# Attention with a running decay: the decay moved into the second score product, the mask into the row minimum

## The chip, the cores and the metric

The kernel runs on one core of a Trainium2 chip. The metric is the device time of one execution in microseconds, lower is better. The profile and the trace come from one execution of the kernel, taken by the hardware profiler. PE is the matrix engine (PEld its weight loads), DVE the vector engine, ACT the scalar engine, POOL is GpSimd, and SP issues DMAs.

## The reference

Attention over 2 batches, 8 heads, 576 positions and 64 channels, with a decay that is summed along the sequence, followed by two mixtures of experts. Only attention is touched by the change:

```python
scores = scale * np.matmul(q, k.transpose(0, 1, 3, 2))
causal = np.triu(np.ones((S, S), dtype=bool), k=1)
cum = np.cumsum(np.maximum(s, 0.0), axis=-1)
bias = -(cum[:, :, :, None] - cum[:, :, None, :])
scores = np.where(causal, -1000000000.0, scores + np.minimum(bias, 0.0))
scores = scores - np.max(scores, axis=-1, keepdims=True)
attn = np.exp(scores)
attn = attn / (np.sum(attn, axis=-1, keepdims=True) + 1e-09)
return np.matmul(attn, v)
...
```

The attention output is then routed to one of 8 experts per token (`_moe_ref`) and goes through 4 dense experts weighted by domain (`_moe2_ref`).

## The kernel before

Attention works in units (h, c, b): head h, block c of 128 queries, batch b. Blocks 0 to 3 see (c + 1) x 128 keys. Block 4 holds the last 64 queries of both batches together, and its 576 keys are cut into two units of 288. That makes 10 units a head and 80 in all, in the order of `ORDER` (`LAST` for head 7).

Everything is kept negated, so the softmax takes a row minimum. Products of float32 accuracy are made from the fast float32r form: q is split into a rounded part and a remainder that stand one above the other in 128 rows (`ql`, turned by PE into `qT`, or `qr` for block 4). k is turned into `kh` (rounded, twice one above the other) and `kl` (what the rounding lost). A unit's scores (`qk`) are two products of 128 rows into one PSUM tile `sc`, `kh` first and `kl` second. A third, bf16 product of an identity with `mkb` or `mrb` adds 1e9 above the diagonal (L209, L218).

The decay is a work of DVE in `nb`: `max(cum_j - cum_i, 0)` per unit from `bc` or `br`, the cumulated row broadcast to all 128 partitions by DMA from the DRAM tensor `ncum_d` (`loadbc`, `loadbr`), and a column per query from `ncT`/`ncR` (L231, L236). For head 0 `bc` is made by PE and ACT instead (L91, L92). `smin` adds scores and decay and takes the row minimum in one DVE instruction (L246). `expo` is the exponential on ACT, `pT` turns the weights on PE and evicts them on ACT to `ptT`, and `av` multiplies them with v (L283, L286, L288). `fin` divides.

The loop in `run` goes over step j and writes the stages of different units: row minimum of unit j+2, turning of j, parts of the next head's preparation (`prep_q`, `prep_k`, `prep_r` at set steps), scores of j+3, exponential of j+1, decay of j+3, value product of j-1. `load(h + 2)` and `loadbc(h + 2)` are written at step 4 of head h. The program's text doesn't fix the order on an engine: a list scheduler puts the instructions into each engine's queue by this order and by when it reckons them ready, and each queue is then worked off in order. `issue_after(x)` is an edge in that ordering, from x to the instructions on x's engine that are written inside it, with no wait on the chip. Buffers: two for scores (`SCB`), three in PSUM for turning (`ps_t`), two for what belongs to a head.

Of the kernel before, what the change touches and what calls it, by code (L numbers as in the profile page):

```python
# [42 lines left out]
class Attention:  # L43
# [6 lines left out]
    def __init__(self, ctx, tc, nc, ident, q, k, v, sp, X):  # L50
        self.tc, self.nc, self.q, self.k, self.v, self.X, self.ident = tc, nc, q, k, v, X, ident
        pool = lambda n, b, **kw: ctx.enter_context(tc.tile_pool(name=n, bufs=b, **kw))
# [3 lines left out]
        dram = pool("adram", 1, space=DRAM)  # L56
# [4 lines left out]
        self.L, self.U, self.last = {}, {}, [None, None]  # L61
# [5 lines left out]
        self.scr = dram.tile([B * H, S], F32, name="ncum_d")  # L67
# [8 lines left out]
        rows = []  # L76
        for b in range(B):
            rows.append(c.tile([16, P], F32, name=f"row{b}"))
            nc.vector.tensor_copy(out=rows[b], in_=ident[:16, 8 * b : 8 * b + 1].to_broadcast([16, P]))
        self.idb = c.tile([P, P], BF16, name="idb")  # L80
        self.ready = nc.vector.tensor_copy(out=self.idb, in_=ident)
        ncm = c.tile([16, S + 64], F32, name="ncm")
        with self.tc.issue_after(self.ready.ins):
            nc.vector.tensor_scalar(out=st, in0=st, scalar1=-1.0, scalar2=0.0, op0=ALU.mult, op1=ALU.min)
        nc.vector.tensor_tensor_scan(out=ncm[:, :S], data0=ones, data1=st, initial=0.0, op0=ALU.mult, op1=ALU.add)
# [3 lines left out]
        for b in range(B):  # L89
# [3 lines left out]
        mk = c.tile([P, P], F32, name="mk")  # L93
        nc.gpsimd.memset(mk, 0.0)
        nc.gpsimd.affine_select(out=mk, in_=mk, pattern=[[-1, P]], compare_op=ALU.is_ge, fill=1e9, base=0, channel_multiplier=1)
        z = c.tile([P, P], F32, name="zz")
        nc.gpsimd.memset(z, 0.0)
        self.mkb = c.tile([P, P], BF16, name="mkb")
        self.mrb = c.tile([P, 64], BF16, name="mrb")
        self.qr = [c.tile([P, 2, P], F32R, name=f"qr{i}") for i in range(2)]  # L100
        with self.tc.issue_after(scan.ins):
            nc.vector.tensor_copy(out=self.mkb, in_=mk)
            nc.vector.tensor_copy(out=self.mrb[0:64, :], in_=mk[0:64, 0:64])
            nc.vector.tensor_copy(out=self.mrb[64:128, :], in_=mk[64:128, 64:128])
            for t in self.qr:
                nc.vector.tensor_copy(out=t, in_=z.unsqueeze(1).to_broadcast([P, 2, P]))
        self.ncT = c.tile([P, 5, 16], F32, name="ncT")
        self.ncR = c.tile([P, 8], F32, name="ncR")
        pt = self.ps_t.tile([P, 512], F32, tag="pt", name="pt")
        for i in range(5):  # L110
            nc.tensor.transpose(out=pt[:, i * 16 : i * 16 + 16], in_=ncm[:, i * P : i * P + P], identity=ident[:16, :16])
        nc.vector.tensor_copy(out=self.ncT, in_=pt[:, :80].rearrange("p (c h) -> p c h", h=16))
        nc.vector.tensor_copy(out=self.ncR[0:64, :], in_=self.ncT[0:64, 4, 0:8])
        nc.vector.tensor_copy(out=self.ncR[64:128, :], in_=self.ncT[64:128, 4, 8:16])

    def warm(self, n):

        t = self.ps_t.tile([P, 512], F32, tag="pt", name="pt")
        for _ in range(n):
# [24 lines left out]
    def loadbc(self, h):  # L144
# [6 lines left out]
        if h:  # L151
            self.loadbr(h)
# [963 lines left out]
```

## Time and profile before

| | us |
|---|---|
| runs, median of 3 (lowest, highest) | 713.06 (712.0, 713.32) |
| the profiled execution, whole | 709.65 |
| its span, first to last instruction | 708.0 |
| PE busy | 682.5 |
| DVE busy | 444.8 |
| ACT busy | 332.1 |
| POOL busy | 166.8 |

The span is what the views of the trace divide up; the whole time has 1.65 us around it. Busy times are sums over the span, and engines work beside each other, so only the one that the others wait for sets the time in a stretch. Attention ends near 155 us, and the two mixtures fill the rest.

### The profile page before, as it was taken

How to read it: one execution, taken by the hardware profiler on the slowest of the kernel's cores; microseconds unless marked ns; L12 is line 12 of the kernel's file. 1: busy time of each engine (PE TensorE's matmuls, PEld its weight loads, DVE VectorE, ACT ScalarE, POOL GpSimd, SP SyncE). 2: the span in 40 equal slices, each digit the busy share in tenths (PEclk: the TensorE clock that was granted, in tenths of full speed). 3: DMA queues.
4: the chain of work that ended last, by engine and by line, in shares of the span. 5: the costliest groups of instructions: out<-in, count | busy, mean ns of one | idle time of the engine just before them, and what ended most of it. 6: DMA issues, size and time to landing. Idle time of an engine off the chain costs nothing.

```text
span 708.0 us, 12759 instructions
## 1 busy us (share of the span) xinstructions
PE 682.5 (96%) x4829; PEld 632.5 (89%) x4830; DVE 444.8 (63%) x1006; ACT 332.1 (47%) x617; POOL 166.8 (24%) x193
## 2 busy tenths in 40 slices
PE   8899999987999999998999999999999999999996
PEld 5789999876999999998989989899899898998995
DVE  7486868653117111367875876868758768687583
ACT  5476777631116111344826636438166364382640
POOL 2000000032400000011513632434126323351333
PEclk9899999978999999999999999999999999999999
DMA  6746557118998977310110111011101100112002
GB/s 139 196 111 187 147 159 172 44 75 267 361 325 293 331 246 236 124 60 4 61 60 1 61 60 32 29 60 61 60 2 60 59 32 29 61 60 60 1 31 104
DMA packets 87015, 78.92 MB, mean 111 GB/s; under 512 B 42699, under 2 KB 67275, under 8 KB 86951
## 3 DMA queue, kind: packets, MB, share of 16 engines
q1 hardware_dynamic: 83063, 72.76, 33.8%
q0 software_dynamic: 1776, 4.79, 1.8%
q10 hardware_dynamic: 2112, 0.52, 0.4%
q8 instruction: 39, 0.64, 0.4%
q14 instruction: 25, 0.20, 0.1%
HBM read 69.08 MB, written 8.99 MB: 110 GB/s over the span
## 4 chain that ended last, share of the span: by engine, by line
PE 51%; issue 1%; DVE 1%; ACT 1%; POOL 0%; POOLq 0%
PE py L1049 15%; PE qa L958 14%; PE qd L958 7%; PE qa L1036 6%; PE qb L958 4%; PE qd L1036 3%; PE qb L1036 1%; DVE acc L1009 1%; ACT hr L981 0%; POOL out_dram L403 0%; ACT hi L872 0%; POOLq L1111 0%; ACT hr L975 0%; DVE acc L1007 0%; DVE sl L873 0%
## 5 line engine op out<-in xcount | busy, mean ns | idle before, releaser
L975 ACT ACTIVATE hr<-qa 128x288 f32<-128x288 f32 x96 | 37.1, 407 | 91.7 <-PE qa L958 91.7
L903 POOL TENSOR_TENSOR wsum<-w 128x512 f32<-128x512 f32 x16 | 24.3, 1529 | 223.3 <-DMA w<-in_moe_w_dram 118.3
L872 ACT ACTIVATE bh<-hr 128x512 fp32r<-128x512 f32 (+1 forms) x72 | 41.2, 585 | 65.0 <-PE py L1049 59.6
L804 PE MATMUL py<-hb,w 128*128 128x128 f32 (+6 forms) x448 | 61.9, 296 | 1.4 <-DMA w<-in_moe_w_dram 1.4
L1049 PE MATMUL py<-hi,bl 128*128 128x512 f32 x160 | 63.0, 394 | 0.0
L1049 PE MATMUL py<-hi,bh 128*128 128x512 f32 x160 | 63.0, 394 | 0.0
L1049 PE MATMUL py<-wl,bh 128*128 128x512 f32 x160 | 63.0, 394 | 0.0
L804 PEld LDWEIGHTS py<-hb,w 128*128 128x128 f32 x448 | 59.6, 190 | 2.0 <-DMA w<-in_moe_w_dram 1.8
L777 PE MATMUL pg<-xs,w 128*128 128x128 f32 (+6 forms) x448 | 59.9, 294 | 0.2 <-ACT xs L753 0.2
L777 PEld LDWEIGHTS pg<-xs,w 128*128 128x128 f32 x448 | 59.0, 190 | 0.3 <-ACT xs L753 0.3
L873 DVE TENSOR_TENSOR bl<-hr,bh 128x512 fp32r<-128x512 f32 (+1 forms) x72 | 56.2, 789 | 1.0 <-ACT bh L872 0.6
L283 PE MATMUL av<-vt,ptT 128*128 128x65 f32 x320 | 48.0, 282 | 0.2 <-ACT ptT L271 0.2
L258 ACT ACTIVATE p<-p,mn 128x512 f32<-128x512 f32 (+4 forms) x72 | 40.6, 582 | 10.2 <-DVE mn L246 9.6
L1009 DVE SCALAR_TENSOR_TENSOR acc<-py,aux,acc 128x512 f32<-128x512 f32 x35 | 26.3, 751 | 29.8 <-PE py L1049 29.8
L873 DVE TENSOR_TENSOR wl<-w,hi 128x1024 fp32r<-128x1024 f32 x32 | 44.7, 1397 | 0.2 <-DVE hr L978 0.2
L283 PEld LDWEIGHTS av<-vt,ptT 128*128 128x128 f32 x320 | 43.3, 201 | 0.7 <-ACT ptT L271 0.5
L271 ACT ACTIVATE ptT<-pt 128x512 f32<-128x512 f32 (+3 forms) x80 | 34.2, 434 | 19.4 <-PE pt L269 19.0
L958 PE MATMUL qa<-xbh,hi 128*128 128x288 f32 x128 | 39.3, 307 | 2.7 <-DVEq L914 2.6
L872 ACT ACTIVATE hi<-wsum 128x1024 fp32r<-128x1024 f32 x32 | 33.0, 1058 | 15.6 <-POOL wsum L868 12.8
L246 DVE CUSTOM_DVE_ANT_0 p<-sc,p 128x512 f32<-128x512 f32 (+4 forms) x72 | 34.5, 484 | 7.1 <-PE sc L209 4.8
L873 DVE TENSOR_TENSOR wl<-wsum,hi 128x1024 fp32r<-128x1024 f32 x32 | 38.9, 1215 | 0.0
L958 PE MATMUL qa<-xth,hi 128*128 128x288 f32 x128 | 37.9, 296 | 0.2 <-ACT hr L975 0.2
(297 smaller groups left out, 2013.7 us busy)
## 6 DMA issues: line engine op xcount, KB each, us to landing
w<-in_moe_w_dram SPq DMA_DIRECT2D x96, 512.0 KB, 6.6
region<-zrow SPq DMA_DIRECT2D x8, 512.0 KB
bc<-ncum_d SPq DMA_DIRECT2D x7, 576.0 KB
ks<-in_k_dram SPq DMA_DIRECT2D x28, 128.0 KB, 3.2
br<-ncum_d SPq DMA_DIRECT2D x16, 144.0 KB, 4.3
qs<-in_q_dram SPq DMA_DIRECT2D x16, 128.0 KB
vt<-in_v_dram SPq DMA_DIRECT2D x16, 128.0 KB, 2.7
xw<-region SPq DMA_DIRECT2D x8, 256.0 KB, 8.6
```

The costliest lines, as they stand in the source:

```text
L246: self.last[1] = nc.vector.tensor_tensor_reduce(out=t[:, lo : lo + w], in0=st["sc"][:, 0:w], in1=t[:, lo : lo + w], scale=1.0, scalar=init ...
L258: self.last[0] = nc.scalar.activation(out=t[:, 0:w], in_=t[:, 0:w], func=AF.Exp, scale=-1.0, bias=st["mn"][:, 0:1])
L271: nc.scalar.activation(out=pt[:r, : n * P], in_=ps[:r, : n * P], func=AF.Copy)
L283: nc.tensor.matmul(out=av[b][:, 65 * c : 65 * c + 65], lhsT=st[("pt", j)], rhs=d["vt"][:, j, b, :], start=j == 0, stop=j == c)
L777: nc.tensor.matmul(out=pg[:, :cap], lhsT=wt[:, cc, fs], rhs=xt[:, cc, :cap], start=i == 0, stop=i == n - 1)
L804: nc.tensor.matmul(out=py[:, :cap], lhsT=wt[:, f % 2, dcs], rhs=ht[:, f, :cap], start=f == 0 and i == 0, stop=f == FC - 1 and i == len(pai ...
L872: nc.scalar.activation(out=hi, in_=t, func=AF.Copy)
L873: nc.vector.tensor_tensor(out=lo, in0=t, in1=hi.bitcast(F32), op=ALU.subtract)
L958: nc.tensor.matmul(out=out[:, :HT], lhsT=a, rhs=b, start=start and n == 0, stop=n == 5, skip_group_check=True)
L975: nc.scalar.activation(out=o, in_=y, func=AF.Copy)
L1036: nc.tensor.matmul(out=q, lhsT=x[:, k, :], rhs=y[:, k, :], start=m == 0 and name not in ACCUMULATED, stop=m == 5, skip_group_check=True)
L1049: nc.tensor.matmul(out=py, lhsT=x[:, f, :], rhs=y[:, f % 2, :], start=f == i == 0, stop=f == 3 and i == 2)
```

## The change

- The decay cum_j - cum_i becomes four further rows of the second score product. `kb` holds the k remainder in rows 0 to 63 and the rows -1, -1 and the rounded and the lost part of the cumulated sum in rows 64 to 67; `q2` (or `r2` for block 4) holds the rounded q in rows 0 to 63 and the matching sums and ones in the other four. The second product thus has 68 rows. It leaves out the product of q's remainder with k's remainder and the clamp at zero, which is only active above the diagonal.
- `nb` computes nothing any more. The broadcast tiles, their DMAs and the tiles for the query side are gone. For a head, `bias` issues two DMAs of two partitions each from the DRAM tensor, and `put_bias` copies them into `kb` (DVE), `q2` (DVE, for head 0 ACT) and `r2` (POOL). This holds for head 0 too.
- The mask product is gone; `smin` adds a constant mask tile `mz` (or `mr`) where it added the decay.
- The rounded q is evicted a second time, to `q2` (`prep_q`) and `r2` (`prep_r`). The k remainder is formed on 64 partitions.
- The scores of a unit are queued on PE behind the last value product written so far (`done`).
- At the start, the rows for the broadcast by PE are gone, the cumulated rows are split by ACT and DVE, and POOL fills the constant tiles.

```diff
-        scan = self.scan = nc.vector.tensor_copy(out=ncm[:, S:], in_=ncm[:, S - 64 : S])
-        nc.sync.dma_start(out=self.scr, in_=ncm[:, :S])
-        self.loadbc(0)
-        for b in range(B):
-            pt = self.ps_t.tile([P, 512], F32, tag="pt", name="pt")
-            nc.tensor.matmul(out=pt, lhsT=rows[b], rhs=ncm[:, 0:512], start=True, stop=True)
-            nc.scalar.activation(out=self.L[0]["bc"][:, b, 0:512], in_=pt, func=AF.Copy)
...
+        self.kb, self.q2, self.r2 = two("kb", 68, (2, S), F32R), two("q2", 68, (8, P), F32R), two("r2", 68, (2, P), F32R)
+        self.sk, self.sq = two("sk", 4, (2, S), F32), two("sq", 4, (2, S), F32)
+        for i in range(2):
+            nc.gpsimd.memset(self.sk[i], -1.0)
+            nc.gpsimd.memset(self.sq[i], 1.0)
...
+        self.scan = nc.vector.tensor_tensor_scan(out=ncm, data0=ones, data1=st, initial=0.0, op0=ALU.mult, op1=ALU.add)
+        self.nl = c.tile([16, 2, S], F32, name="nl")
+        nc.scalar.activation(out=self.nl.bitcast(F32R)[:, 0], in_=ncm, func=AF.Copy)
+        nc.vector.tensor_tensor(out=self.nl.bitcast(F32R)[:, 1], in0=ncm, in1=self.nl[:, 0], op=ALU.subtract)
...
+        self.scr = dram.tile([2, 8, 2, S], F32, name="ncum_d")
+        nc.sync.dma_start(out=self.scr.rearrange("b h a n -> (b h) a n"), in_=self.nl)
+        self.bias(0), self.put_bias(0), self.bias(1), self.put_bias(1)
...
-            nc.sync.dma_start(out=bc, in_=self.scr.rearrange("(b h) n -> h b n", b=2)[h].unsqueeze(0).to_broadcast([P, 2, S]))
...
+    def bias(self, h):
+
+        nc, src = self.nc, self.scr[:, h].rearrange("b a n -> a b n")
+        nc.sync.dma_start(out=self.sk[h % 2][0:2], in_=src)
+        (nc.sync if h else nc.scalar).dma_start(out=self.sq[h % 2][2:4], in_=src)
+
+    def put_bias(self, h):
+        nc, i = self.nc, h % 2
+        nc.vector.tensor_copy(out=self.kb[i][64:68], in_=self.sk[i])
+        q2 = self.q2[i][64:68].rearrange("p (b c) t -> p b (c t)", b=2)
         if h:
+            nc.vector.tensor_copy(out=q2, in_=self.sq[i][:, :, 0:512])
+        else:
+            nc.scalar.activation(out=q2, in_=self.sq[i][:, :, 0:512], func=AF.Copy)
         for b in range(B):
+            nc.gpsimd.tensor_copy(out=self.r2[i][64:68, b, 64 * b : 64 * b + 64], in_=self.sq[i][:, b, 512:576])
...
+        nc.scalar.activation(out=d["q2"][0:64, 4 * g : 4 * g + 4, :], in_=pt[0:64].rearrange("p (c t) -> p c t", c=4), func=AF.Copy)
...
-        nc.vector.tensor_tensor(out=d["kl"][:, g, 0:512], in0=pt, in1=d["kh"][:, g, 0:512].bitcast(F32), op=ALU.subtract)
+        nc.vector.tensor_tensor(out=d["kb"][0:64, g, 0:512], in0=pt[0:64], in1=d["kh"][0:64, g, 0:512].bitcast(F32), op=ALU.subtract)
...
+        for b in range(B):
+            nc.scalar.activation(out=d["r2"][0:64, b, 64 * b : 64 * b + 64], in_=pt[0:64, 64 * b : 64 * b + 64], func=AF.Copy)
...
-            for i, kt in enumerate((d["kh"], d["kl"])):
-                nc.tensor.matmul(out=sc[:, 0:w], lhsT=d["qT"][:, 4 * b + c, :], rhs=kt[:, b, 0:w], start=i == 0, stop=False)
-            nc.tensor.matmul(out=sc[:, w - P : w], lhsT=self.idb, rhs=self.mkb, start=False, stop=True)
+            for i, (qt, kt) in enumerate(((d["qT"], d["kh"]), (d["q2"], d["kb"]))):
+                nc.tensor.matmul(out=sc[:, 0:w], lhsT=qt[:, 4 * b + c, :], rhs=kt[:, b, 0:w], start=i == 0, stop=i == 1)
...
-            nc.vector.tensor_scalar(
-                out=t[:, 0:w], in0=d["bc"][:, b, 0:w], scalar1=self.ncT[:, c, 8 * b + h : 8 * b + h + 1], scalar2=0.0,
-                op0=ALU.subtract, op1=ALU.max,
-            )
...
+        mask = self.mz[:, 512 - w :] if c < 4 else self.mr if b else self.mz[:, 0:288]
...
-            out=t[:, lo : lo + w], in0=st["sc"][:, 0:w], in1=t[:, lo : lo + w], scale=1.0, scalar=init,
+            out=t[:, lo : lo + w], in0=st["sc"][:, 0:w], in1=mask, scale=1.0, scalar=init,
...
-        self.load(1), self.loadbr(0), self.loadbc(1)
+        self.load(1)
...
-                self.qk(at(j + 3))
+                with self.tc.issue_after(self.done.ins) if self.done else ExitStack():
+                    self.qk(at(j + 3))
...
                 if pos == 4:
-                    self.load(h + 2), self.loadbc(h + 2)
+                    self.bias(h + 2), self.load(h + 2)
...
                 elif pos == 9:
+                    self.put_bias(h + 2)
                     self.prep_split(h + 2)
```

## Rows read from the trace of the kernel before

**Rows 1.** The page: busy us, share of the span, instructions of each engine.
```profile
PE 682.5 (96%) x4829; PEld 632.5 (89%) x4830; DVE 444.8 (63%) x1006; ACT 332.1 (47%) x617; POOL 166.8 (24%) x193
```
**Rows 2.** Windows: stretch, its length, busy us by engine, clock, DMA.
```profile
core 0: us, PE busy (x) PEld busy (x) DVE busy (x) ACT busy (x) POOL busy (x), PEclk, DMA share, GB/s
12.19:35.34 23.15, 18.69 (x124) 16.21 (x123) 12.81 (x47) 12.27 (x27) 0.00 (x0) 0.85 0.68 179
67.02:82.26 15.24, 15.02 (x129) 13.61 (x128) 12.41 (x46) 11.22 (x26) 0.23 (x2) 1.00 0.64 170
...
22.00:25.50 3.50, 0.71 (x5) 0.56 (x4) 1.63 (x6) 0.63 (x2) 0.00 (x0) 1.00 0.99 214
25.50:32.40 6.90, 6.68 (x31) 5.82 (x29) 3.13 (x13) 3.58 (x8) 0.00 (x0) 0.51 0.68 161
```
**Rows 3.** Timeline of DVE in head 0: start, us, line, idle before and its releaser.
```profile
23.87 0.49 DVE L231 TENSOR_SCALAR p<-bc,ncT 128x512 f32<-128x512 f32 x1 [3.19 <-DMA bc<-ncum_d]
```
**Rows 4.** Groups by form on PE, 0 to 160: busy us, mean ns, idle before.
```profile
L283 PE MATMUL av<-vt,ptT 128*128 128x65 f32 x320 | 48.0, 282 | 0.2 <-ACT ptT L271 0.2
...
L209 PE MATMUL sc<-mkb,idb 128*128 128x128 bf16 x64 | 14.8, 231 | 0.0
```
**Rows 5.** Timeline of PE in settled heads: start, us, line, shapes.
```profile
64.43 0.21 PE L218 MATMUL sc<-mrb,idb 128*128 128x64 bf16 x1
64.47 0.64 PE L283 MATMUL av<-vt,ptT 128*128 128x65 f32 x4
...
65.62 0.40 PE L208 MATMUL sc<-kl,qT 128*128 128x512 f32 x1
65.86 0.23 PE L209 MATMUL sc<-mkb,idb 128*128 128x128 bf16 x1
65.93 0.83 PE L283 MATMUL av<-vt,ptT 128*128 128x65 f32 x6
...
128.49 0.29 PE L213 MATMUL sc<-kl,qr 128*128 128x288 f32 x1
128.62 0.78 PE L283 MATMUL av<-vt,ptT 128*128 128x65 f32 x6
```
**Rows 6.** Timeline of PE around two groups of the experts' transposes.
```profile
213.56 0.81 PE L728 MATMUL tp<-ident,xw 120*128 120x120 f32 x6
214.21 0.29 PE L804 MATMUL py<-hb,w 128*128 128x144 f32 x1
...
289.67 1.85 PE L728 MATMUL tp<-ident,xw 128*128 128x128 f32 x8
291.45 0.41 PE L804 MATMUL py<-hb,w 128*128 128x172 f32 x1
```
**Rows 7.** Groups on DVE: the decay instructions, and a cast at the start.
```profile
L231 DVE TENSOR_SCALAR p<-bc,ncT 128x512 f32<-128x512 f32 (+2 forms) x64 | 23.3, 383 | 15.2 <-PE pt L269 6.5 <-ACT xt L492 4.7 <-DMA bc<-ncum_d 3.2
...
L236 DVE TENSOR_SCALAR p<-br,ncR 128x576 f32<-128x576 f32 x8 | 4.2, 520 | 2.0 <-DMA br<-ncum_d 1.8
...
L106 DVE CAST qr<-zz 128x256 fp32r<-128x256 f32 x2 | 0.5, 288 | 0.0
```
**Rows 8.** Groups by form on ACT: two evictions.
```profile
L179 ACT ACTIVATE qT<-pt 128x512 fp32r<-128x512 f32 x16 | 9.5, 596 | 4.1 <-PE pt L178 4.1
...
L271 ACT ACTIVATE ptT<-pt 64x128 f32<-64x128 f32 x8 | 2.2, 270 | 1.8 <-PE pt L269 1.7
```
**Rows 9.** Timeline of the start: start, us, engine (SPq issues DMAs), line.
```profile
3.52 1.34 DVE L85 TENSOR_TENSOR_SCAN ncm<-ones,st 16x576 f32<-16x576 f32 x1
...
7.40 0.69 SPq L141 DMA_DIRECT2D vr<-in_v_dram  x1
...
10.49 0.42 SPq L87 DMA_DIRECT2D ncum_d<-ncm  x1
...
11.91 0.48 PE L208 MATMUL sc<-kl,qT 128*128 128x512 f32 x1
...
16.16 1.24 SPq L157 DMA_DIRECT2D br<-ncum_d  x2
```
**Rows 10.** DMA issues by line, 0 to 25: KB each, median us to landing.
```profile
ncum_d<-ncm SPq DMA_DIRECT2D x1, 36.0 KB, 2.2
```

More of the change, by code (lines that the diff above doesn't have):

```diff
@@ L75, in __init__ @@
         self.warm(10)
-        rows = []
-        for b in range(B):
[L78 to L82, printed above, removed]
+        two = lambda n, p, w, t: [c.tile([p, *w], t, name=f"{n}{i}") for i in range(2)]
@@ L83, in __init__ @@
+        self.qr = two("qr", P, (2, P), F32R)
+        self.kb, self.q2, self.r2 = two("kb", 68, (2, S), F32R), two("q2", 68, (8, P), F32R), two("r2", 68, (2, P), F32R)
[3 more added lines that the diff above has]
+            nc.gpsimd.memset(self.sq[i], 1.0)
+        self.ready = nc.vector.memset(ones[:, 0:1], 1.0)
+        ncm = c.tile([16, S], F32, name="ncm")
         with self.tc.issue_after(self.ready.ins):
@@ L96, in __init__ @@
         z = c.tile([P, P], F32, name="zz")
         nc.gpsimd.memset(z, 0.0)
[L98 to L113, printed above, removed]
@@ L114, in __init__ @@
-        nc.vector.tensor_copy(out=self.ncR[64:128, :], in_=self.ncT[64:128, 4, 8:16])
+        zz = z.unsqueeze(1).to_broadcast([P, 2, P])
+        for i in range(2):
+            nc.gpsimd.tensor_copy(out=self.r2[i], in_=zz[0:68])
+            nc.gpsimd.tensor_copy(out=self.qr[i], in_=zz)
+        self.scr = dram.tile([2, 8, 2, S], F32, name="ncum_d")
+        nc.sync.dma_start(out=self.scr.rearrange("b h a n -> (b h) a n"), in_=self.nl)
+        self.bias(0), self.put_bias(0), self.bias(1), self.put_bias(1)
@@ new lines, in __init__ @@
+        self.mz = c.tile([P, 512], F32, name="mz")
+        nc.gpsimd.memset(self.mz, 0.0)
+        nc.gpsimd.affine_select(
+            out=self.mz[:, 384:512], in_=self.mz[:, 384:512], pattern=[[-1, P]], compare_op=ALU.is_ge, fill=1e9, base=0, channel_multiplier=1
+        )
+        self.mr = c.tile([P, 288], F32, name="mr")
+        nc.gpsimd.memset(self.mr, 0.0)
+        for b in range(B):
+            r = slice(64 * b, 64 * b + 64)
+            nc.gpsimd.tensor_copy(out=self.mr[r, 224:288], in_=self.mz[r, 384 + 64 * b : 448 + 64 * b])
@@ L197, in prep_r @@
         nc.vector.tensor_copy(out=d["qr"][:, 1, 64:128], in_=pt[:, 64:128])
-        nc.vector.tensor_tensor(out=d["kl"][:, :, 512:576], in0=kp, in1=d["kh"][:, :, 512:576].bitcast(F32), op=ALU.subtract)
+        for b in range(B):
+            nc.scalar.activation(out=d["r2"][0:64, b, 64 * b : 64 * b + 64], in_=pt[0:64, 64 * b : 64 * b + 64], func=AF.Copy)
+        nc.vector.tensor_tensor(out=d["kb"][0:64, :, 512:576], in0=kp[0:64], in1=d["kh"][0:64, :, 512:576].bitcast(F32), op=ALU.subtract)
     def qk(self, u):
@@ L287, in av @@
             for j in range(4):
-                nc.tensor.matmul(out=o, lhsT=st[("pt", j)], rhs=d["vt"][:, j].rearrange("p b d -> p (b d)"), start=False, stop=j == 3)
+                self.done = nc.tensor.matmul(out=o, lhsT=st[("pt", j)], rhs=d["vt"][:, j].rearrange("p b d -> p (b d)"), start=False, stop=j == 3)
     def fin(self, h, b, c0, c1):
```

38 lines of the change are left out of this document (7 added, 31 removed).

## The prediction

> **What bounds the kernel now.** I read the engine totals first, then the windows, and then the timeline of PE alone. The totals [rows 1] put PE at 96% of the span, but that is an average, and a busy PE may be a PE that waits inside its pipeline, so the attention stage has to be looked at by itself. The windows [rows 2] compare the stretch between the last key evictions of two heads. A settled head takes 15.24 us with PE busy for 15.02 of it at full clock, DVE for 12.41 and ACT for 11.22. So from the second head on PE sets the pace, and ACT has 4.0 us a head to spare. The first head is another matter: 23.15 us for about the same number of matmuls, at a mean clock of 0.85. That is 7.9 us lost. The same rows show where: between 22.0 and 25.5 PE is busy for 0.71 us, and from 25.5 to 32.4 it works at a granted clock of 0.51 (the 1.2 GHz level), which costs 6.9 x 0.49 = 3.4 us. The wait before it is DVE's: its decay instruction of the next head stands 3.19 us for the broadcast of the decay rows [rows 3], the row minimum queued behind it on DVE is late, and PE's scores wait for their buffer. 2.8 + 3.4 leaves 1.7 us for filling the pipeline.
>
> What comes after attention is the same code in both kernels and starts from attention's result, so I take attention's difference as the kernel's.
>
> **The mask product.** 64 of 72 unit masks are 128 columns wide [rows 4], the other 8 are 64. What one costs is not its 231 ns of duration, which is mostly pipeline, but what it adds between its neighbours' starts. In [rows 5] the second score product of 512 columns starts at 65.62, its mask at 65.86 and the value product at 65.93: 0.07 us for the mask. The narrow one sits at 64.43 with the next start at 64.47: 0.04 us. That the product ahead does not simply get longer when the mask is gone is seen where there is none: a 288-column second product starts at 128.49 and the value product at 128.62, 0.13 us for 288 columns against the 0.24 for 512 ahead of the wide mask, the same per column. 64 x 0.07 + 8 x 0.04 = 4.8 us. One head of eight is not set by PE, so I count seven eighths: **-4.2 us**. The mask is now the second operand of the minimum, where the decay tile was, so DVE's instruction keeps its shape.
>
> **68 rows in the second product.** The second product loads 68 rows of weights, where it loaded 128. The trace has no 68. Its nearest rows on either side [rows 6]: six transposes in a row, of 120 and of 128 rows, take 213.56 to 214.21, 0.11 us each, which is the pace of full ones. Eight that alternate 60 and 128 take 289.67 to 291.45, 0.22 us each. (That merged row names one form; in the code four of the eight have 60 rows, the 188 of that expert's share less 128.) So a change to 60 rows and one back each cost 0.11 us, and a change to 120 costs none. The Trainium skill says why that may be, in "TensorEngine Tiling (Array Packing)", Key Properties and Available Configurations: the array is cut into tiles of 128, 64 or 32 rows, and changing the mode drains it. By that rule 68 rows fit no smaller tile than 128, and the sum would be as with 120 rows. Both bounds stay: 0, or 64 units x 2 changes + 16 calls x 4 changes = 192 changes x 0.114 us (0.222 less the 0.108 of the other group) = 22 us. 68 is nearer to 60 in count. But the loss is a step and no share: of what 60 rows lose nothing at all is left at 120, and I put the step at half the array, so that 68 lies with 120. I take 0, and give the other side a chance of its own.
>
> **DVE.** It loses the decay instructions: 64 of 383 ns and 8 of 520 ns [rows 7], 3.6 us a head. It gains two copies a head of 4 x 1152 and 4 x 1024. The nearest row is a cast of 256 columns at 288 ns [rows 7]: between that and 4.5 times it, so 0.6 to 2.5 us a head. DVE is relieved either way, and it is not the bound. The most that an earlier minimum gives back is what PE idles in a settled head, 15.24 - 15.02 = 0.22 us, for seven heads 1.5 us. I take 0. The key remainder keeps its columns on half the partitions, and its time.
>
> **ACT.** Each query group now leaves PSUM twice, and two 64-column copies are added: 2 x 0.596 + 2 x 0.27 at most [rows 8] = 1.7 us a head, on 4.0 us of spare time. Cover holds on average, but these copies stand in the queue ahead of exponentials and of the evictions that value products wait for, and hold a transpose buffer longer. If a head shows one such copy, 0.6 us x 7 = 4.2 us; if all is covered, 0. I take +0.5, because the value products waited for ACT for 0.2 us in all [rows 4] with 4 us a head to spare, and 2.3 remain.
>
> **Score products behind value products.** The edge keeps a unit's scores from being issued ahead of the last value product written before it. It adds no work; a late eviction by ACT now holds the scores too. Its price is in ACT's bound. POOL's two small copies a head stand behind the memsets of the value tiles, which wait for the head before; they are wanted a head later. On SP two small DMAs take the place of three broadcast ones, in front of the next loads.
>
> **The start.** Before, the decay reached the first units from SBUF through PE and ACT; the trip through DRAM was only for later. Now no unit is complete before the cumulated rows have been written to DRAM and read back into four partitions, and copied. In [rows 9] the scan ends at 3.52 + 1.34 = 4.86; SP issues the first head's loads until 7.40 + 0.69 = 8.09, and the write only at 10.49, behind loads of the second head. The first complete second product starts at 11.91. The new write needs one ACT copy and one DVE subtraction more, some 0.7 us each by the 512-column eviction [rows 8]: issue at 11.9. It lands 2.2 us later [rows 10], the read back takes as long again, 16.3, and the copies 0.7: **17.0**, 5.1 us later than 11.91. Bounds: the write goes out at 8.09, and the copies take 0.3: 12.8, 0.9 later. Or the reads go out behind all of the second head's loads, where the old reads went, at 16.16 [rows 9], and with 3 us for landing and 0.65 for the copy make 19.8, 7.9 later. On ACT the first query-side read is queued too, and ACT's evictions behind it wait with it.
>
> Against that goes the 2.8 us stall for the broadcast, which can't occur any more. The cold stretch stays in some form: PE now idles at the start for about as long as it did at 22. I take 2.6 us for it (1.7 to 3.4, half or all of what it was), and the fill of 1.7 as before. New loss 5.1 + 1.7 + 2.6 = 9.4 against 7.9: **+1.5 us**. Bounds: 0.9 + 1.7 + 1.7 = 4.3, so -3.6; 7.9 + 1.7 + 3.4 = 13.0, so +5.1.
>
> **Sum.** -4.2 + 0.5 + 1.5 = -2.2 us: a span of 708.0 would become 705.8, and the profiled execution of 709.65 would take 707.4. The median of the runs, 713.06, is 3.4 us above that execution, and I take the difference over unchanged: 713.06 - 2.2 = **710.9**.
>
> **The rivals.**
> *A quick start.* The write goes out right after the first loads, and the stall is pure gain: -4.2 + 0.5 - 3.6 = -7.3, 705.8. For it: removing three large broadcasts clears SP and the queues. Against: SP was busy with loads of the next head when the row was ready.
> *The start eats the gain (other side).* The reads stand behind the second head's loads: -4.2 + 0.5 + 5.1 = +1.4, 714.5. For it: the old write was 5.6 us later than its data. It decides against the gain from about 3.7 us of net start loss, that is when the first complete product starts after 19. Here is the price of giving up the path through PE.
> *ACT becomes the bound.* +4.2 from it: -4.2 + 4.2 + 1.5 = +1.5, 714.6. For it: 1.7 us in bursts; against it: 2.3 us a head still spare.
> *68 rows cost a change each way.* -4.2 + 0.5 + 1.5 + 22 = +19.8, 732.9. For it: the 60-row transposes; against it: the 120-row ones.
>
> **How the numbers follow.** A measurement here can tell about 0.2%, 1.4 us, from no change. Chances: my sum 0.40 (its own range 708.5 to 713: mostly faster, a third within 0.2%), quick start 0.22, slow start 0.20 (half same, half slower), ACT 0.12 (mostly slower), 68 rows 0.06. So faster 0.48, same 0.28, slower 0.24. The range takes the bounds: low -4.2 - 1.5 - 3.6 = -9.3, 703.8; high +5.1 (ACT and mid-start, or slow start with part of ACT), 718.2; the last rival lies outside.
>
> **What would show it.** In the profile after: second product to value product 0.24 us apart at 512 columns and no mask between (else the mask was hidden); a settled head near 14.7 us with PE above 98% of it; PE's waits still naming no ACT (else the ACT rival). The start: the first second product at about 17, and a stretch at the 1.2 GHz level behind it, then nothing like the stall at 22. It is wrong if second products stand 0.1 us or more apart from their neighbours beyond their columns, or if the first one starts before 14 or after 19.

## The result, and the profile after

The changed kernel took 718.98 us (median of 10 runs, 715.85 to 723.6), the kernel before 715.39 us (10 runs, 712.0 to 716.21). The ratio is 1.0066, with a 95% interval of 1.0045 to 1.0087: **slower, by about 4.7 us** (the two medians lie 3.6 apart), where 710.9 us and a gain had been forecast. The profiled execution took 718.49 us, with a span of 716.4 (before: 709.65 and 708.0) at a mean granted clock of 0.972 (before 0.981). The profile before is faster than each of its kernel's ten runs, so the two profiles lie further apart than the kernels.

In the page of the changed kernel the totals answer to [rows 1]. The columns are the same: busy us, share, instructions.

```profile
PE 680.8 (95%) x4748; PEld 634.8 (89%) x4749; DVE 429.8 (60%) x939; ACT 341.3 (48%) x649; POOL 178.4 (25%) x220
```

PE (TensorE) and DVE are busy for less, as forecast, ACT for 9 us more and POOL for 12. So the loss has to be looked for in stretches. A head's stretch is cut as in [rows 2], at the eviction of its last 64 keys of each batch (line 195 in both kernels, called the head's remainder below), and heads are counted from 0. The windows of the changed kernel, with the columns of [rows 2]:

```profile
15.79:35.29 19.50, 18.25 (x112) 16.25 (x113) 11.31 (x40) 13.26 (x32) 0.64 (x3) 0.77 0.30 67
49.80:73.62 23.82, 20.43 (x147) 19.43 (x145) 11.36 (x40) 14.20 (x32) 0.67 (x4) 0.86 0.42 119
55.90:58.02 2.12, 0.00 (x0) 0.03 (x1) 1.93 (x7) 1.12 (x2) 0.00 (x0) 1.00 0.67 162
59.02:65.85 6.83, 6.26 (x31) 6.04 (x29) 1.16 (x3) 3.35 (x8) 0.00 (x0) 0.50 0.69 165
73.62:88.42 14.80, 14.17 (x120) 13.49 (x118) 10.52 (x40) 11.46 (x29) 0.65 (x4) 1.00 0.40 94
```

The last row is the settled head that stood at 15.24 us in [rows 2]: 0.44 us shorter, with PE 0.85 us less busy. The second row is the loss. From head 2's remainder to head 3's, a stretch that also holds products of the router, the kernel before took 18.19 us and this one 23.82:

```profile
48.83:67.02 18.19, 18.08 (x156) 16.70 (x155) 12.23 (x46) 12.48 (x28) 0.21 (x2) 1.00 0.65 174
```

In it PE now does nothing for 2.12 us, and then works 6.83 us at a granted clock of 0.50, the 1.2 GHz level. The first row shows that the start too runs far below full clock: 0.77 over 19.5 us.

The table below puts attention together from four cuts in each trace: the remainder evictions of head 1 and head 3, and the first transposes of the first MoE layer. The third column thus holds the rest of the router too, and the last column goes from those transposes to the first product of the second MoE layer. "Before, again" and "after, again" are later runs of the unedited kernels, told of below.

| trace | start to head 1 | head 1 to 3 | head 3 to MoE | first MoE layer |
|---|---|---|---|---|
| before | 35.3 | 31.7 | 95.0 | 161.9 |
| before, again (`e9_before_again`) | 34.4 | 31.7 | 93.8 | 170.3 |
| after | 35.3 | 38.3 | 91.4 | 166.2 |
| after, again (`e5_after_again`) | 37.4 | 36.5 | 91.4 | 169.8 |
| after, in the same order (`e7_split_early`) | 37.5 | 36.5 | 91.6 | 167.5 |

By the means, the change costs 1.9 us up to head 1, **costs 5.4 us from head 1 to head 3**, and gains 3.0 us from there to MoE. That is +4.3, beside a measured 4.7; the traces of one kernel differ among themselves by up to 2.3 us in each of these columns.

The gain doesn't lie where the forecast put it. The four heads from head 3's remainder to head 7's, before and after:

```profile
67.02:126.41 59.39, 58.85 (x495) 53.55 (x494) 45.46 (x171) 43.41 (x98) 0.86 (x8) 1.00 0.64 170
73.62:132.72 59.10, 56.45 (x468) 53.46 (x467) 39.01 (x146) 47.52 (x114) 2.27 (x14) 1.00 0.39 103
```

PE has 2.4 us less to do, 0.6 us a head as forecast, but the time falls by 0.3 us: PE now stands idle for 2.65 us, where it was 0.54. In this stretch it waits for DVE's scaling of a finished output and for ACT's second eviction:

```profile
PE av L276 <- DVE X L288: 1.9, 3, 0.6
PE pt L185 <- ACT q L179: 0.6, 1, 0.6
```

The other 2.7 of the 3.0 us are gained behind head 7's remainder (35.7 and 34.4 us in the traces before, 32.2 to 32.5 after).

PE's four longest waits from 16 to 160 us of the trace after (us in total, times, the longest):

```profile
PE pt L177 <- DVE ql L164: 2.8, 2, 2.1
PE pt L185 <- ACT q L179: 2.4, 4, 0.6
PE av L276 <- DVE X L288: 2.1, 4, 0.6
PE sc L210 <- DVE kb L149: 1.5, 1, 1.5
```

In the kernel before PE waited 0.2 us for the query remainder, and for the other three not at all. The longest wait of its own in attention, 2.8 us behind the broadcast in head 0, is gone. The longest new one is in PE's timeline, here with two second score products (`sc<-kb`) in settled work:

```profile
31.90 0.40 PE L210 MATMUL sc<-kb,q 68*128 68x512 f32 x1
32.14 0.67 PE L273 MATMUL av<-vt,ptT 128*128 128x65 f32 x5
...
47.55 0.30 PE L214 MATMUL sc<-kb,r 68*128 68x288 f32 x1
47.68 0.56 PE L273 MATMUL av<-vt,ptT 128*128 128x65 f32 x4
...
55.61 0.28 PE L210 MATMUL sc<-kb,q 68*128 68x256 f32 x1
58.03 0.63 PE L177 MATMUL pt<-ident,ql 128*128 128x128 f32 x4 [2.14 <-DVE ql L164]
```

The products of 68 rows cost no step: the next instruction starts 0.24 us behind 512 columns and 0.13 behind 288, as with 128 rows in [rows 5]. But at 55.6 PE has come to the query transposes of head 3 and waits for DVE's half of the split queries. What DVE did in the meantime:

```profile
51.20 0.75 DVE L149 CAST kb<-sk 4x1152 fp32r<-4x1152 f32 x1
...
52.62 0.69 DVE L152 CAST q<-sq 4x1024 fp32r<-4x1024 f32 x1
53.34 0.69 DVE L236 CUSTOM_DVE_ANT_0 p<-sc,mz 128x512 f32<-128x512 f32 x1
...
57.12 0.76 DVE L164 SCALAR_TENSOR_TENSOR ql<-qs,ql 128x576 fp32r<-128x576 f32 x1
```

The two row copies of the change stand ahead of it, then the row minima of the next units, and the split comes last. ACT's half of the split, which DVE's needs, is late as well; it stands behind two exponentials that waited for those minima:

```profile
54.07 1.01 ACT L248 ACTIVATE p<-p,mn 128x512 f32<-128x512 f32 x2 [1.47 <-DVE mn L236]
54.99 0.67 ACT L163 ACTIVATE ql<-qs 128x576 fp32r<-128x576 f32 x1
```

The loads are not what it waits for: ACT's half starts with no idle time in front of it. In the kernel before, ACT's half started at 50.62 and DVE's at 51.56, right behind it.

The start, as it answers to [rows 9] (SPq and ACTq issue DMAs):

```profile
8.91 0.43 SPq L99 DMA_DIRECT2D ncum_d<-nl  x1
11.51 0.63 SPq L144 DMA_DIRECT2D sk<-ncum_d  x2
11.54 0.57 ACTq L145 DMA_DIRECT2D sq<-ncum_d  x1
12.15 0.60 ACT L178 ACTIVATE qT<-pt 128x512 fp32r<-128x512 f32 x1 [4.10 <-POOL vr L135]
12.80 0.90 PE L210 MATMUL sc<-kh,qT 128*128 128x512 f32 x2 [3.33 <-ACT qT L178]
...
14.74 0.75 DVE L149 CAST kb<-sk 4x1152 fp32r<-4x1152 f32 x1
...
15.64 0.77 PE L210 MATMUL sc<-kb,q 68*128 68x512 f32 x1 [1.51 <-DVE kb L149]
```

The row is written at 8.91 and read at 11.5, earlier than forecast, and the first second product starts at 15.64. But ACT stands idle for 4.10 us. The view names a memset of POOL for it, which runs from 12.00 to 12.10. It isn't the reason: in `e4_read_by_sp`, below, that memset comes as late (12.12), and ACT doesn't stand. ACT's own queue holds the DMA of 11.54, which reads what the write of 8.91 has yet to land, and the query evictions stand behind it. So PE waits 3.33 us, does two products and two transposes, and waits 1.51 us more.

### The profile page after: what moved, and what is told of

It is laid out like the page before. It is cut to its first block, busy times and chain, and to the rows that moved or that the text cites. A ratio compares the mean times of both kernels' runs of the same rounds, so it can differ in the third digit from the quotient of the medians.

```text
span 716.4 us, 12567 instructions
## 1 busy us (share of the span) xinstructions
PE 680.8 (95%) x4748; PEld 634.8 (89%) x4749; DVE 429.8 (60%) x939; ACT 341.3 (48%) x649; POOL 178.4 (25%) x220
## 4 chain that ended last, share of the span: by engine, by line
PE 49%; issue 1%; POOL 1%; DVE 1%; ACT 1%; POOLq 0%; ACTq 0%
PE qa L950 14%; PE py L1041 14%; PE qd L950 7%; PE qa L1028 5%; PE qb L950 4%; PE qd L1028 3%; PE qb L1028 1%; DVE acc L1001 1%; POOL wsum L858 0%; ACT hr L973 0%; POOL out_dram L395 0%; ACT hi L864 0%; POOL wsum L857 0%; POOL wsum L860 0%; POOL wsum L859 0%
## 5 line engine op out<-in xcount | busy, mean ns | idle before, releaser
L769 PE MATMUL pg<-xs,w 128*128 128x128 f32 (+6 forms) x448 | 62.2, 301 | 2.5 <-issue 2.3
L769 PEld LDWEIGHTS pg<-xs,w 128*128 128x128 f32 x448 | 60.8, 196 | 3.2 <-issue 2.9
L236 DVE CUSTOM_DVE_ANT_0 p<-sc,mz 128x512 f32<-128x512 f32 (+4 forms) x72 | 34.0, 483 | 28.4 <-PE sc L210 20.3
L273 PEld LDWEIGHTS av<-vt,ptT 128*128 128x128 f32 x320 | 44.9, 201 | 2.7 <-ACT ptT L261 1.2
L273 PE MATMUL av<-vt,ptT 128*128 128x65 f32 x320 | 46.2, 275 | 1.1 <-issue 0.7
L950 PE MATMUL qa<-xbl,hi 128*128 128x288 f32 x128 | 38.2, 298 | 0.0
```

The lines of the kernel that those rows point to most:

```text
L236: self.last[1] = nc.vector.tensor_tensor_reduce(out=t[:, lo : lo + w], in0=st["sc"][:, 0:w], in1=mask, scale=1.0, scalar=init, op0=ALU.add ...
L273: self.done = nc.tensor.matmul(out=av[b][:, 65 * c : 65 * c + 65], lhsT=st[("pt", j)], rhs=d["vt"][:, j, b, :], start=j == 0, stop=j == c)
L769: nc.tensor.matmul(out=pg[:, :cap], lhsT=wt[:, cc, fs], rhs=xt[:, cc, :cap], start=i == 0, stop=i == n - 1)
L950: nc.tensor.matmul(out=out[:, :HT], lhsT=a, rhs=b, start=start and n == 0, stop=n == 5, skip_group_check=True)
```

## The experiments

Each ratio is against the kernel before on the same chip, with its 95% interval. Theories are named in the expectations; A and B are told in the first four. C and S: the change has made the work smaller, and the loss is PE's waits at the start (C) and at one head's query transposes (S), each with time at 1.2 GHz behind it. W: the work itself is dearer. Some expectations call the late head "head 2"; the rows above show that it is head 3, with the wait between the remainders of head 2 and head 3.

**The same kernels again.** `e5_after_again` is the changed kernel, `e9_before_again` the kernel before, neither edited.

> The changed kernel once more, unedited, on the chip of the three runs beside it. Theory C (the engines' work did shrink, and the loss is time of TensorE at 1.2 GHz behind its own idle waits): ratio 1.0066 again within 0.002; its granted clock 0.008 to 0.012 below that of the kernel before on the same chip; and time x granted clock (the time that the run would take at 2.4 GHz throughout, as far as TensorE sets it) 1 to 4 us below that of the kernel before. Rival W (the work itself became dearer): the same ratio, clocks of both kernels within 0.003 of each other, and time x clock 3 us or more above.

Measured: 1.0076 (1.0047 to 1.0104). The granted clock is 0.970 by the median of the runs, against 0.982 before; the product of each run's time and clock has the medians 699.2 and 702.1 us, 2.9 lower after the change. By these signs C holds and W falls: there is less work, and it takes longer.

> The kernel before, unedited, for a trace from the same chip as the runs beside it. If the late start of one expert's products in the first MoE layer (2 to 4 us of TensorE idle some 25 us after that layer begins, which the changed kernel's traces show on two chips and those of four runs on a third do not) belongs to the chip, it stands in this trace too when the others of this call have it, and MoE's first layer then takes the same time from its first transposes to the second layer's first product, within 3 us. If it belongs to the change, this trace has 161.9 us there (within 1) and the others of this call 166 or more. Ratio 1.000 within 0.002 either way.

Measured: 0.999 (0.9963 to 1.0017). The late start is there, on the kernel without the change (PE's timeline, first MoE layer):

```profile
182.03 2.50 PE L804 MATMUL py<-hb,w 128*128 128x128 f32 x20
190.11 2.18 PE L777 MATMUL pg<-xs,w 128*128 128x136 f32 x8 [5.58 <-ACT xs L731]
```

Its first MoE layer takes 170.3 us. In the traces of `e1` to `e4`, which have the change, the layer takes 161.4 to 162.9 us. So the 4.3 us that separate the first two traces in that layer (161.9 and 166.2) are not shown to be the change's.

**DVE's copies, the edge, the second eviction.** Three single edits of the changed kernel, on one chip with `e4_read_by_sp`:

```diff
# e1_rows_by_pool
-        nc.vector.tensor_copy(out=self.kb[i][64:68], in_=self.sk[i])
+        (nc.gpsimd if h > 1 else nc.vector).tensor_copy(out=self.kb[i][64:68], in_=self.sk[i])
...
-            nc.vector.tensor_copy(out=q2, in_=self.sq[i][:, :, 0:512])
+            (nc.gpsimd if h > 1 else nc.vector).tensor_copy(out=q2, in_=self.sq[i][:, :, 0:512])
# e2_no_edge
-                with self.tc.issue_after(self.done.ins) if self.done else ExitStack():
-                    self.qk(at(j + 3))
+                self.qk(at(j + 3))
# e3_q2_by_dve
-        nc.scalar.activation(out=d["q2"][0:64, 4 * g : 4 * g + 4, :], in_=pt[0:64].rearrange("p (c t) -> p c t", c=4), func=AF.Copy)
+        nc.vector.tensor_copy(out=d["q2"][0:64, 4 * g : 4 * g + 4, :], in_=pt[0:64].rearrange("p (c t) -> p c t", c=4))
```

> From head 2 on, the two copies of the decay rows into the products' operands go to POOL instead of DVE. Theory A (in the settled heads the copies on DVE, 0.75 and 0.69 us, stand at each head's turn in front of row minima and of the eviction of the finished output): PE's waits of 0.63 us for that eviction (three in the changed kernel's trace) go, and so does the wait of 2.14 us ahead of head 2's query transposes together with the 6.8 us at the 1.2 GHz level behind it: 3 to 8 us less than the changed kernel, a ratio to the kernel before of 0.996 to 1.002. Theory B (the loss is the start's): the same as the changed kernel within 0.2%, ratio 1.005 to 1.009.

Measured: 1.0091 (1.0059 to 1.0122). The wait for DVE's query remainder stands, with 2.5 us: it is not the length of the copies. DVE's queue without them:

```profile
56.68 0.32 DVE L297 TENSOR_SCALAR r<-av 64x1 f32<-64x1 f32 x2 [2.23 <-PE av L278]
...
58.32 0.42 DVE L236 CUSTOM_DVE_ANT_0 p<-sc,mz 128x256 f32<-128x256 f32 x1
...
59.05 0.76 DVE L164 SCALAR_TENSOR_TENSOR ql<-qs,ql 128x576 fp32r<-128x576 f32 x1 [0.30 <-ACT ql L163]
```

DVE has idle time here, and the split still stands behind the row minima of scores that PE has only just made (the last at 57.17). So it is the place of the split in the queues that makes it late.

> The edge that queues a unit's scores behind the last value product is left out. If the edge costs (scores held up by a late eviction): 1 to 3 us less than the changed kernel, ratio 1.002 to 1.005. If the edge helps (without it scores crowd out the transposes that exponentials and evictions wait for): 1 to 4 us more, ratio 1.008 to 1.012. Theories A and B both expect neither: within 0.2%, and a stall at some head's turn as before.

Measured: 1.0055 (1.0031 to 1.0080). PE's waits for the query remainder fall to 0.5 us in all; in their place it waits 2.1 us for row minima, in seven pieces. From head 2 to head 3 it still takes 21.98 us, and the time is not told apart from the changed kernel's.

> The second eviction of the turned queries goes to DVE instead of ACT. The changed kernel's trace has four waits of PE of 0.6 us in front of the key transposes, for a transpose buffer that ACT's second eviction still holds. If ACT is what is short: these waits go, 2 to 2.5 us less, ratio 1.003. If DVE's queue at the head's turn is what is short (theory A): no gain or 1 to 3 us more, ratio 1.006 to 1.011. Theory B: within 0.2% of the changed kernel.

Measured: 1.0079 (1.0051 to 1.0107). PE's waits for the second eviction go, and the wait for DVE's remainder is 2.5 us. So taking the second evictions of `q2` off ACT gains nothing. The edit puts them on DVE, so it doesn't price them alone.

**The start.** `e4_read_by_sp` takes the first read off ACT's queue:

```diff
-        (nc.sync if h else nc.scalar).dma_start(out=self.sq[h % 2][2:4], in_=src)
+        nc.sync.dma_start(out=self.sq[h % 2][2:4], in_=src)
```

> For head 0 the query side's rows are read by a DMA on SP's queue instead of ACT's. In the changed kernel ACT stands from 8.05 to 12.15 behind that DMA issue, which waits for the write to DRAM. Theory B (the start sets the loss, and the held ACT is part of it): first complete product at 15.0 or earlier instead of 15.64, fewer microseconds at the 1.2 GHz level than the 13.65 behind 11.2, 2 to 5 us less than the changed kernel, ratio 1.000 to 1.004. Theory A: the first complete product waits for the rows all the same, within 0.2%, ratio 1.005 to 1.009.

Measured: 1.0037 (1.0005 to 1.0069), from 704.8 to 714.7 us in twelve runs; the interval overlaps that of the changed kernel. ACT no longer stands, head 0's remainder is evicted at 10.42 in place of 15.79, and head 1's at 32.46. `e6_fill` adds eight products of zeros behind head 0's transposes to that edit, `e11_start_filled` fourteen (and the steps of `e10_queries_late`):

```diff
+        self.warm(8)
         self.load(1)
```

> The read of the second small tile on SyncE's queue (as in e4_read_by_sp), and eight products of zeros with zeros (128x512, bf16) queued on TensorE behind the first head's transposes, where it stood idle for 1.6 and 3.1 us in e4_read_by_sp while the decay rows were on their way. They change no output. Theory C: the cold stretch at about 13 us goes, and with it the upper group of times of e4_read_by_sp (712 to 715); against e4_read_by_sp's 1.0037 the ratio falls to about 1.000 (0.998 to 1.002). Rival W: idle time filled with nothing gives nothing, ratio 1.003 to 1.005, or more if the eight products (0.21 us each at 2.4 GHz, 0.43 at 1.2) come to stand before the first second product.

Measured: 1.0026 (1.0005 to 1.0047). A stretch of 10.24 us at 1.2 GHz from 17.35 is left, and head 1's remainder comes at 34.85: not shown to be better than without the zeros.

> The edits of e4_read_by_sp (read on SyncE's queue) and e10_queries_late, and fourteen products of zeros in the hole of the start (six of them ahead of the product that waits for VectorE at about 11.7 us, eight behind it). Theory C (the loss of the change is time at 1.2 GHz that idle TensorE brings on): TensorE is idle for under 1 us in any one piece from 4 us to head 1's remainder eviction, the sum at 1.2 GHz before MoE falls from 27 to 31 us to 14 to 20, and the ratio is 0.992 to 0.998. Rival W (the work is dearer, the clock beside the point): 1.002 or more.

Measured: 0.997 (0.993 to 1.0011). Up to head 1's remainder, at 31.03, there is no time at 1.2 GHz; but the wait for head 3's queries is longer (3.27 us), since the steps that were moved are head 2's.

In the kernel before, the ten products of zeros at the very start are taken away:

```diff
         nc.vector.memset(self.wz, 0.0)
-        self.warm(10)
```

> The kernel before without the ten products of zeros at its start: the work that counts is the same, and TensorE is idle for 2 to 4 us more before head 0's transposes, which wait for the loads in either case. Theory C (idle TensorE at the start costs by the clock behind it): granted clock 0.003 to 0.010 lower, more time at 1.2 GHz before head 1's remainder eviction, ratio 1.002 to 1.008. Rival W: ratio 0.998 to 1.002, the idle time lay beside the loads.

Measured: 1.0004 (0.9975 to 1.0033). Here C misses. PE's timeline of that run:

```profile
9.13 1.11 PE L184 MATMUL pt<-ident,ks 128*128 128x128 f32 x4
10.04 1.06 PE L177 MATMUL pt<-ident,ql 128*128 128x128 f32 x4
10.89 1.06 PE L184 MATMUL pt<-ident,ks 128*128 128x128 f32 x4
11.79 0.69 PE L177 MATMUL pt<-ident,ql 128*128 128x128 f32 x4
```

Until 11.8 the first transposes run slow, four in 1.06 us, where `e9_before_again` has 0.60; but in the first trace of the kernel before, zeros and all, they take 1.06 us too. The first second product starts at 12.69 in place of 11.6 to 11.9, and head 1's remainder comes at 34.03, no later than in the two traces of the kernel before. So PE's idle time ahead of the first work costs nothing that can be told apart here. What costs, in the other traces, is a wait in the midst of the work.

**The order.** Three edits of what is written when:

```diff
# e7_split_early (and two buffers for ql)
+                elif pos == 8:
+                    self.prep_split(h + 2)
                 elif pos == 9:
                     self.put_bias(h + 2)
-                    self.prep_split(h + 2)
# e10_queries_late
-                    steps = FIRST if h == 0 else STEPS
+                    steps = FIRST if h == 0 else [2, 3, 4, 6, 8] if h == 1 else STEPS
# e13_load_first
                 if pos == 4:
-                    self.bias(h + 2), self.load(h + 2)
+                    self.load(h + 2), self.bias(h + 2)
```

> Only the queue order and buffers at the change of heads: the split of the head-after-next's queries is issued one unit earlier, ahead of the row copies, into a second buffer. The work is the same. Theory S (the 2.1 us stall of TensorE at head 2's query transposes and the 6.8 us at 1.2 GHz behind it are one loss of about 5 us): no wait of over 1 us there, the time from head 1's to head 2's remainder eviction falls from 23.8 to 18 to 19 us, ratio about 0.999 (0.997 to 1.002). Rival (the queries are just the first in a line of late things, the second eviction and the row copies hold TensorE next): the wait goes to another line within head 1, the time between the remainder evictions stays over 21 us, ratio 1.005 to 1.008.

Measured: 1.0058 (1.0034 to 1.0081). The order of the queues came out as it was, so this is the changed kernel once more and tells nothing of S.

> One edit in the order of TensorE's queue: head 2's steps move back by two units and one, so that its query transposes stand behind two more products and four transposes than in the changed kernel, where they held the queue for 2.1 us (the earlier try, e7_split_early, left the queues' order as it was). Theory S (that stall and the time at 1.2 GHz behind it are one loss): no wait of over 0.7 us at those transposes, head 1's remainder eviction to head 2's takes 18 to 20 us in place of 22 to 24, and the ratio falls by 0.004 to 0.008 from the changed kernel's 1.0066 to 1.0076, to 0.999 to 1.003. Rival (the stall only moves on, to what then comes late): 22 us or more between the two, ratio 1.005 or above.

Measured: 1.0074 (1.0047 to 1.0101). The stretch from head 1 to head 2 fell to 13.16 us (14.51 after the change), that from head 2 to head 3 rose to 25.15, with a wait of 3.37 us. The edit was one head too early; S is not tested by it.

> One swap: a head's loads are issued ahead of its two small decay DMAs (as the kernel before does with its broadcasts), in place of behind them. In the queues, VectorE's query remainder of head 3 then stands ahead of the row copies and of two row minima. Theory S (the 2.1 us wait at those transposes, 23.8 us from head 2's remainder eviction to head 3's against 18.2 before, comes from that order): no wait of over 1 us there, 18 to 20.5 us between the two evictions, ratio 0.003 to 0.008 below the changed kernel's 1.0066 to 1.0076, that is 0.999 to 1.004. Rival: the wait stands as it was or goes to another line, 22 us or more, ratio 1.005 or above.

Measured: **1.0015 (0.9991 to 1.0039)**. With the loads first, ACT's half of the split starts at 51.35, and DVE's stands ahead of the row copies and of the next row minima:

```profile
52.05 0.76 DVE L164 SCALAR_TENSOR_TENSOR ql<-qs,ql 128x576 fp32r<-128x576 f32 x1 [1.17 <-ACT ql L163]
...
55.12 0.75 DVE L149 CAST kb<-sk 4x1152 fp32r<-4x1152 f32 x1
```

and PE goes from the score product straight into the transposes:

```profile
53.55 0.28 PE L210 MATMUL sc<-kb,q 68*128 68x256 f32 x1
53.67 0.60 PE L177 MATMUL pt<-ident,ql 128*128 128x128 f32 x4
```

From head 2 to head 3 it takes 18.99 us, from head 1 to head 3 31.4 (changed kernel 36.5 to 38.3), with no time at 1.2 GHz between. S holds. The granted clock of the whole run stays at 0.970 by the median, as in `e5_after_again`, so that the gain doesn't show in it. Some of it is given back: 92.2 us from head 3 to MoE, where it was 91.4, with the settled head at 15.03.

**The mask.** `e12_mask_product` puts the mask products back (those of the last block too); the minimum adds zeros in place of the mask.

```diff
+            nc.tensor.matmul(out=sc[:, w - P : w], lhsT=self.idb, rhs=self.mkb, start=False, stop=True)
...
-        mask = self.mz[:, 512 - w :] if c < 4 else self.mr if b else self.mz[:, 0:288]
+        mask = self.z0[:, 0:w]
```

> The mask goes back into the scores: the changed kernel with the mask products on TensorE as in the kernel before (72 in all, bf16), while the row minimum adds a tile of zeros, at the same cost on VectorE. By the price of the forecast (4.2 us over all heads, no drain) the ratio rises by 0.006 to 1.0125 to 1.0135, and a plain settled head goes from 14.79 to about 15.25 us. Rival (those products lay in TensorE's slack, and their removal gained nothing): the ratio stays at 1.0066 to 1.0076.

Measured: 1.0145 (1.0113 to 1.0178), 0.007 to 0.009 above the runs of the changed kernel, or 5 to 6 us. A plain settled head, in windows:

```profile
106.37:122.10 15.73, 15.49 (x129) 13.73 (x127) 10.31 (x40) 12.09 (x29) 1.24 (x4) 1.00 0.45 121
```

0.94 us longer than the same stretch of the changed kernel (14.79, PE busy for 14.15). Over the four heads from head 3's remainder to head 7's it is 0.7 us a head (61.8 us against 59.1), where the forecast had 0.6. The price is confirmed; by the ratio it was low, though the intervals don't exclude it, and the plain head of 15.73 was expected at 15.25. One thing more moved with this edit: the wait for head 3's queries is 0.7 us in it.

**Together.** `e8_all` is `e6_fill` with `e7_split_early`; `e14_start_and_load` has the swap, the read on SyncE's queue and fourteen products of zeros; `e15_and_no_edge` drops the edge too.

> Read on SyncE's queue, eight products of zeros at the start, and the early split together. Theories C and S: the gains add, ratio 0.992 to 0.997, granted clock at or above that of the kernel before. Rival W: 1.002 or more.

Measured: 1.0024 (0.9999 to 1.0048), like `e6_fill`, as the order of the queries did not move in it either.

> The swap of e13_load_first, the read on SyncE's queue (e4_read_by_sp) and the fourteen products of zeros in the hole of the start (e11_start_filled). Theories C and S: TensorE's time at 1.2 GHz before MoE is 10 to 17 us as in the kernel before (13.7 to 23.9), and the ratio is 0.990 to 0.997. Rival W (the work is dearer): 1.000 or more.

Measured: **0.9947 (0.9917 to 0.9978)**, 711.01 us against 714.32: faster than both kernels. PE at its start:

```profile
10.17 1.46 PE L117 MATMUL pt<-wz 128*128 128x512 bf16 x6
11.58 0.19 PE L463 MATMUL pl<-neb,oneb 1*128 1x72 bf16 x1
11.70 1.90 PE L117 MATMUL pt<-wz 128*128 128x512 bf16 x8
14.73 0.56 PE L210 MATMUL sc<-kb,q 68*128 68x512 f32 x2 [1.14 <-ACT q L154]
```

and its windows from head 0's remainder to head 1's, and on to head 3's:

```profile
10.40:30.96 20.56, 17.98 (x127) 14.17 (x126) 12.36 (x44) 14.52 (x33) 2.62 (x22) 1.00 0.45 99
30.96:62.35 31.39, 29.73 (x252) 28.64 (x250) 20.29 (x77) 24.20 (x58) 1.38 (x8) 1.00 0.50 113
```

Full clock throughout, and MoE's first transposes start at 154.5 us (before 162.1 and 159.9, after 165.0 to 165.6).

> The edits of e14_start_and_load, and the score products without the edge that holds them back behind value products. If the edge hurts (e2_no_edge was 0.001 better than the changed kernel, within the intervals), the ratio is 0.001 to 0.003 below that of e14_start_and_load; if it helps in the settled heads, as much above.

Measured: 0.9956 (0.9917 to 0.9994): with and without the edge is not told apart.

## Why the prediction was wrong, step by step

**"On SP two small DMAs take the place of three broadcast ones, in front of the next loads": this is the step that failed.** It was counted at nothing. With the two DMAs ahead of the loads, both halves of the query split, which takes what the loads bring, stand later in their queues: ACT's behind exponentials, DVE's behind the row copies and the minima of the next units, and PE waits at the transposes. Measured: 5.1 us from head 1 to head 3 (36.5 in `e5_after_again` against 31.4 with the calls swapped, in `e13_load_first` and in `e14_start_and_load`). Of these 2.1 lie before head 2's remainder, where head 2's split is late by 0.7, and 3.0 behind it, with the wait of 2.1. The row copies alone are not the reason, since with them off DVE (`e1_rows_by_pool`) the wait was 2.5. The forecast named the place and weighed the work of the copies ("DVE is relieved either way"), and did not ask which instruction comes late when the loads do. None of its rivals was this one. That the swapped calls move the split in both queues is shown; why the order follows from them stays open.

What the clock adds to this wait is seen from head 2 to head 3 in traces that all have it, with 2.1 us. It takes 20.97 us in `e4_read_by_sp`, where no time at 1.2 GHz follows, 21.97 in `e5_after_again`, with 3.4 us of it, and 23.82 in the first trace, with 6.83 (23.69 and 24.11 in `e6_fill` and `e8_all`). With the calls swapped it takes 18.99:

```profile
46.98:67.95 20.97, 17.54 (x147) 16.59 (x145) 11.36 (x40) 13.87 (x32) 0.67 (x4) 1.00 0.49 137
51.94:73.91 21.97, 19.06 (x147) 17.94 (x145) 11.36 (x40) 13.99 (x32) 0.67 (x4) 0.92 0.46 130
47.81:66.80 18.99, 17.33 (x147) 16.56 (x145) 10.79 (x42) 13.76 (x33) 0.61 (x4) 1.00 0.43 105
```

By these traces the late split costs 2.0 us by itself, and the clock behind it nothing to 3 us more.

**The start: right in size, by another road, and so by luck.** +1.5 us forecast, +1.9 measured up to head 1. The first second product started at 15.64, within the bounds of 12.8 to 19.8, and the stall at 22 is gone. The sentence that ACT's evictions wait behind the first read stood there without a price, and it is the larger part by the traces: with the read on SyncE's queue head 1's remainder came at 32.5, 34.9 and 34.4 us (the last two with eight products of zeros as well), against 35.3, 37.4 and 37.5. The cold stretch that "stays in some form" was taken at 2.6 us, as half to all of what it was; it is 13.65 us long in the trace after and 17.07 in the two repeats, where 6.9 stood in [rows 2] and 3.4 in the second trace before. With the hole filled and the read moved, the start is 31.0 us, 3.4 to 4.4 less than before: the rival of a quick start, at 3.6, was within reach and not what the change did.

**The mask: right in PE's work, but most of it was not kept in the settled heads.** -4.2 us forecast, or 0.6 us a head. PE's busy time falls by just that over four heads (58.85 to 56.45 us), and the time by 0.3, since new waits take the rest. Putting the mask back cost 5 to 6 us by the ratios.

**68 rows: right.** In the rows shown there is no step beyond the columns; the bound of 22 us is gone. The Trainium skill lists, in "TensorEngine Tiling (Array Packing)", Available Configurations, tiles of 128, 64 and 32 rows. By that list 68 rows would take the same tile as 128, which the page doesn't say of itself; the 0.24 us agree with it.

**DVE and ACT: too low.** A settled head takes 14.80 us, as forecast (14.7), but PE is busy for 14.17 of it, 96% and not above 98: at changes of head it waits 0.6 us for DVE's output scaling (2.1 us in all, counted at 0) or for ACT's second eviction (2.4 us in all, counted at 0.5). The price at ACT was taken from the 0.2 us of [rows 4]; PE's waits for the exponential, 0.9 us in the kernel before, were left out. The rival in which ACT becomes the bound is not borne out: with the evictions of `q2` off ACT the ratio was 1.0079.

**"What comes after attention is the same code": holds** as far as the traces tell, but not by one pair of them, where the first MoE layer differs by 4.3 us. It took a second trace of the kernel before, in which that layer takes 170.3 us.

The sum, with the measured terms: +1.9 at the start, +5.4 from head 1 to head 3, -3.0 after it: +4.3 us, against -2.2.

## What to carry to other kernels

When a change puts new transfers ahead of old ones, look at the instructions that take what the old ones bring, ask where the scheduler now puts them, and who waits for them; the work can shrink on the engine that sets the pace and the time still grow. Look at the order in the queues before and after, and not only at the busy times. A wait of two microseconds in the midst of PE's work cost nothing to 3 us more in the clock behind it, so price a wait and its slow stretch as one. And a DMA that has to wait should not be issued from the queue of an engine whose next instruction is wanted.

## What the runs showed of the hardware

- A DMA issued on ACT's queue, which had to wait for another DMA's landing, held ACT for 4.10 us; with it on SyncE's queue ACT did not stand. The view put the wait down to a memset of POOL that ended 0.05 us before ACT went on.
- The same wait of PE, 2.1 us at the same place, was followed by no time at 1.2 GHz in `e4_read_by_sp`, by 3.4 us in two traces and by 6.8 in three.
- A second product of 68 rows between products of 128 rows costs no more than its columns (0.24 us at 512), while 60-row transposes between full ones had cost 0.11 us a change [rows 6].
- The granted clock that the windows give for the start is not always that of the work: in `e16_before_cold_start` it is 1.00 up to 13.01 us, while transposes at 9 to 11.8 us took 1.06 us for four, as against 0.69 at 11.8, and 0.60 in `e9_before_again`.
- In the first MoE layer of `e9_before_again` PE is idle for 5.58 us, at 385 GB/s of DMA, for an operand whose transposes the trace shows done 8 us earlier; in five traces (the first of the kernel before, and those of `e1` to `e4`) there is no such wait. What holds the operand is left open.
